# Two output halves in two groups of PSUM partitions, or as alternate rows of one eight-lane sum: a decode block on one core

## The chip, the cores and the metric

The kernel runs on one core of a Trainium2 chip. The metric is the device time of one execution in microseconds; several executions are timed and their median is given. A profiled execution of the same program gives the trace from which the views below are read.

## What is computed

Four sequences each decode one token. The input x (4 x 640) is layer-normalized, goes through an attention block with a cache and through a gated MLP, and both results are added to x:

```python
xn = _layernorm(x)
# A: 32 heads of 128, 4096 cached positions for each of the 4 sequences
q = (xn @ wq)                                   # 640 x 4096
scores = einsum('bhqd,bhkd->bhqk', q, k_cache) * Dh ** -0.5
o = einsum('bhqk,bhkd->bhqd', softmax(scores), v_cache)
a = o.reshape(B, 1, 4096) @ wo                  # 4096 x 640
# B: F = 1728, Fh = 864
z = gelu(xn @ w_in)
g = w_sp * layernorm(z[..., Fh:]) + b_sp
b = (z[..., :Fh] * g) @ w_out                   # 864 x 640
out = x + a + b                                 # 4 x 640, bf16
```

All inputs are bf16. The two caches hold 134 MB each, so 282 MB are read for 5 KB of result.

## The kernel before

**Units.** The attention is cut into 16 units: four groups of eight heads (HG = 4), and four sequences in each. Unit u is group u // 4, sequence u % 4. A unit's K, 8.4 MB, is spread over 128 partitions and loaded in four quarters (NK = 4, a quarter is 64 rows of 128 on each partition); its V, again 8.4 MB, goes to one tile, v_all. K quarters live in a ring of seven places, k_ring. The projection weights wo of a head group (1.3 MB) are loaded into place 4 of that ring.

**One K quarter** (step n of 64) is multiplied by the broadcast query on VectorE (`product`, L514), folded once (`fold_half`, L520), summed further on TensorE by eight matmuls with the identity (`sums`, L529), and reduced on VectorE (`row_sums`, L542). After four quarters come the maximum (`head_max`, L551 to L558), the exponential on ScalarE (`exps`, L564) and the spreading of the weights by head (`by_head`, L575). The product with V is 64 matmuls for each unit (`weighted`, L599), their result is copied by ScalarE (`take`, L611) and sorted (`pick_unit`, L630).

**The order of the loads** is a list written out by hand. `pump()` issues them one after another on SP's queue as soon as the place that a load goes to has been given back; the code marks a place as busy or free when the instructions that use it have been put down, and the semaphores that follow from it are waited for by SP. The order of instructions on TensorE, VectorE, ScalarE and SP in the main part is that of the program; nothing is reordered.

**The output sum.** All contributions to the output are accumulated in one PSUM tile, out_ps, in one bank: x itself (two matmuls, L355), the MLP (`gmlp`, 20 matmuls at L480, ten terms in two halves of 320 columns, at step 2 of 64), and wo (`group_proj`, 16 matmuls at L668 for each of the four head groups, eight heads in two halves). A half is 320 of the 640 output columns. Half 0 is summed in partitions 0 to 3, half 1 in partitions 32 to 35, each with a stationary operand of four columns, one for each sequence.

**The end.** After the last unit's K comes its V in two parts: the first through `weighted`, the second directly as stationary operand, 128 small matmuls (L778), in four pieces that arrive one after the other. Then VectorE divides by the sums (L786, into o_n_last), `group_proj` adds the last eight heads, whose wo arrives in six pieces (heads 0 and 1, 2 and 3, 4 and 5, 6, and the two halves of 7), ScalarE copies out_ps to SBUF as bf16 (L792), and two stores of four rows of 640 bytes go out, one on ScalarE's queue (L793), one on SP's (L794).

Of the kernel before, what the change touches and what calls it, by code (L numbers as in the profile page):

```python
# [9 lines left out]
FP32 = mybir.dt.float32  # L10
BF16 = mybir.dt.bfloat16
ACT = mybir.ActivationFunctionType
ALU = mybir.AluOpType
# [4 lines left out]
def kernel(  # L18
# [14 lines left out]
    nc = tc.nc  # L33
    P = nc.NUM_PARTITIONS
    Bsz, Sq, D = A_x.shape
# [12 lines left out]
    NQ = P // QD  # L48
    HT = 8
    PAR = HT // NQ  # L50
    LN = P // HT
    HG = H // HT
# [12 lines left out]
    NFC = NFF + FR  # L65
    LS = 5
    NOH = D // 2
# [4 lines left out]
    JR = Dh // QH  # L72
# [5 lines left out]
    const = ctx.enter_context(tc.tile_pool(name="const", bufs=1))  # L78
    work = ctx.enter_context(tc.tile_pool(name="work", bufs=1))
    small = ctx.enter_context(tc.tile_pool(name="small", bufs=2))  # L80
    once = ctx.enter_context(tc.tile_pool(name="once", bufs=1))
# [5 lines left out]
    ps_out = ctx.enter_context(tc.tile_pool(name="ps_out", bufs=1, space=PSUM))  # L87
# [133 lines left out]
    ident = const.tile([P, P], BF16)  # L221
# [3 lines left out]
    for e in range(PAR):  # L225
        nc.gpsimd.tensor_copy(
            out=of_row[:, e, :, :, e, :],
            in_=ident[:].rearrange("p (k q) -> p q k", q=QD)[:, 0:Bsz, :, None].to_broadcast(
                [P, Bsz, NQ, LN]
            ),  # L230
# [15 lines left out]
    for i in range(NSTAT):  # L246
# [5 lines left out]
        out=rstd[:], in_=mv[:, 1:2], func=ACT.Sqrt, bias=eps_tile[:Bsz], scale=1.0  # L252
# [4 lines left out]
        out=xn_bf[:],  # L257
        in0=x_bf[:],
# [11 lines left out]
    for c in range(DC):  # L270
        nc.tensor.transpose(
            out=xnT_ps[:, c, :], in_=xn_v[:, c, :], identity=ident[:Bsz, :Bsz]
# [8 lines left out]
    for e in range(PAR):  # L281
        q_ps = ps_pv.tile([P, HG, Dh], FP32, tag="pv", name="q_ps")
        for c in range(DC):
            for k in range(NQ):
                nc.tensor.matmul(  # L285
                    out=q_ps[k * QD : (k + 1) * QD],
# [58 lines left out]
        op1=ALU.add,  # L345
    )

    out_ps = ps_out.tile([P, NOH], FP32)
    OG = 32

    def out_sum(half):
        return out_ps[OG * half : OG * half + Bsz, :]

    for half in range(2):
        nc.tensor.matmul(  # L355
            out=out_ps[OG * half : OG * half + OG, :],
            lhsT=ident[:Bsz, :OG],
            rhs=x_bf[:, half * NOH : (half + 1) * NOH],
            start=True,
            stop=False,  # L360
        )

# [4 lines left out]
    nc.gpsimd.memset(gm["zz"][:], 0.0)  # L367
    gm["st"] = work.tile([1, 5 * Bsz], FP32, name="st")
    gm["ac"] = work.tile([1, 2 * Bsz], FP32, name="ac")
    gm["yT"] = work.tile([P, NFC, Bsz], BF16, name="yT")  # L370

    def gmlp():
        zz, gw, gt, gz = (gm[n] for n in ("zz", "gw", "gt", "gz"))
# [97 lines left out]
            in1=ac_sb[:, None, Bsz : 2 * Bsz].to_broadcast([P, NFC, Bsz]),  # L471
            op=ALU.add,
        )
        nc.vector.tensor_tensor(out=gm["yT"][:], in0=gz[:, 0, :, :], in1=sq, op=ALU.mult)
        w_terms = [w_out_sb[:, k] for k in range(NV)] + [w_row_sb]
        w_terms += [w_end_sb[:FT, r] for r in range(FR)]
        for k in range(NFC):
            w = P if k < NFF else FT
            for half in range(2):
                nc.tensor.matmul(  # L480
                    out=out_sum(half),
                    lhsT=gm["yT"][:w, k, :],
                    rhs=w_terms[k][:, half * NOH : (half + 1) * NOH],
                    start=False,
                    stop=False,
                )
# [151 lines left out]
    def group_turn(hg):  # L638
        rden = small.tile([P, 1], FP32, name="rden")
        nc.vector.reciprocal(out=rden[:], in_=rdens.pop(hg)[:])  # L640


        o_q = gr.pop(hg)[:].rearrange("p (q j) -> p q j", j=JR)
        o_n = once.tile([P, JR, PAR, QH], BF16, name="o_n")
        for e in range(PAR):
            nc.vector.scalar_tensor_tensor(  # L646
                out=o_n[:, :, e, :].rearrange("p j q -> p q j"),
                in0=o_q,
                scalar=rden[:, 0:1],
                in1=of_set[:, e : e + 1, None].to_broadcast([P, QH, JR]),  # L650
                op0=ALU.mult,
                op1=ALU.mult,
            )
        o_t = once.tile([P, JR, QD], BF16, name="o_t")
        nc.vector.transpose(
            out=o_t[:].rearrange("p j q -> p (j q)"),
            in_=o_n[:].rearrange("p j e q -> p (j e q)"),
        )
        o_s = once.tile([P, JR, Bsz], BF16, name="o_s")
        nc.vector.tensor_tensor(  # L660
            out=o_s[:], in0=o_t[:, :, 0:Bsz], in1=o_t[:, :, Bsz : 2 * Bsz], op=ALU.add
        )
        gr[hg] = [o_s[:, j, :] for j in range(JR)]

    def group_proj(hg):
        for n, o in enumerate(gr.pop(hg)):
            for half in range(2):
                nc.tensor.matmul(  # L668
                    out=out_sum(half),
                    lhsT=o,  # L670
                    rhs=wo_sb[:, n, half * NOH : (half + 1) * NOH],
                    start=False,
                    stop=(hg == HG - 1 and n == HT - 1),
                )
        busy.remove(WO_AT)

# [25 lines left out]
    with tc.manual_schedule(engines={E.PE, E.DVE, E.Activation, E.SP}):  # L702
        stage_q(0)
        nc.scalar.dma_start(out=wsp_bf[:], in_=B_w_sp[0:1, 0:1])
        nc.scalar.dma_start(out=bsp_bf[:], in_=B_b_sp[0:1].rearrange("(a b) -> a b", a=1))
        waiting = None
        mlp = gmlp()
        for n in range(NK * NU):
            u, i = divmod(n, NK)
            product(n)  # L710
            if n in (1, 2):
                next(mlp)
            if n:
                row_sums(n - 1)
            if i == 0 and u:
                head_max(u - 1)
                if waiting in taken:
                    picked(waiting)
            fold_half(n)
            if n == 1:  # L720
                next(mlp)
            if n in (1, 2):
                next(mlp)
            if i == 0 and u:
                exps(u - 1)
                if waiting in pvs:
                    take(waiting)
                by_head(u - 1)
            sums(n)
            if i == 0 and u + 1 < NU:  # L730
                stage_q(u + 1)
            if i == 0 and waiting is not None:
                if waiting in taken:
                    picked(waiting)
                if waiting % Bsz == Bsz - 1:
                    group_turn(waiting // Bsz)
                    group_proj(waiting // Bsz)
                waiting = None
            if n == 0:
                next(mlp)  # L740
            if n == 2:
                busy.remove(V)
            if n in turns:
                w = waiting = turns[n]
                if w % Bsz == Bsz - 1:
                    group_den(w // Bsz)
                if w == NU - 3:
                    weighted(w, v_runs[:, 0:NC], more=True)
                    weighted(w, v_runs[:, NC:NR], NG // 2)
                else:  # L750
                    weighted(w, v_runs)
                if i < NK - 1:
                    take(w)
                busy.remove(V)
            pump()
        weighted(NU - 2, v_runs)
        row_sums(NK * NU - 1)
        head_max(NU - 1)
        exps(NU - 1)
        take(NU - 2)  # L760
        by_head(NU - 1)
        den = ps_m.tile([P, NQ, PAR, Bsz], FP32, tag="m", name="den_all")
        nc.tensor.matmul(
            out=den[:],
            lhsT=ones_sq[:],
            rhs=acc[(HG - 1) % NACC][:, :, 0 : PAR * Bsz],
            start=True,
            stop=True,
        )
        rden = small.tile([P, NQ, PAR, Bsz], FP32, name="rden_all")  # L770
        nc.vector.reciprocal(out=rden[:], in_=den[:])
        picked(NU - 2)
        u, b = NU - 1, Bsz - 1
        weighted(u, v_ends[0])
        take(u)
        pick_last(u, more=True)
        for c in range(NC):
            nc.tensor.matmul(  # L778
                out=o_last[0][:, :, :, b],
                lhsT=v_ends[1][:, c, :],  # L780
                rhs=p_m[:, u % 2, NG // 2 + c // CB, c % CB, :].rearrange("p (k e) -> p k e", e=PAR),
                start=False,
                stop=(c == NC - 1),
            )
        o_n = small.tile([P, NQ, PAR, Bsz], BF16, name="o_n_last")
        nc.vector.tensor_tensor(out=o_n[:], in0=o_last[0][:], in1=rden[:], op=ALU.mult)  # L786
        gr[HG - 1] = [o_n[:, h // PAR, h % PAR, :] for h in range(HT)]
        group_proj(HG - 1)

        res = work.tile([P, NOH], BF16, name="res")  # L790
        out_v = out.flatten_outer_dims()
        nc.scalar.copy(out=res[0 : OG + Bsz], in_=out_ps[0 : OG + Bsz])  # L792
        nc.scalar.dma_start(out=out_v[:, 0:NOH], in_=res[0:Bsz])  # L793
        nc.sync.dma_start(out=out_v[:, NOH:D], in_=res[OG : OG + Bsz])  # L794


# [28 lines left out]
```

## Time and profile before

| | |
|---|---|
| median of 3 runs | 662.36 us (662.22 to 663.16) |
| span of the profiled execution | 660.5 us; the page gives no time outside the span |
| granted TensorE clock, mean | 0.694 |
| TensorE busy with matmuls | 310.9 us (47%) |
| VectorE busy | 524.9 us (79%) |
| bytes moved by DMA | 282.56 MB, mean 428 GB/s |
| L668 in the tail | 16 matmuls, 654.73 to 657.64 us |
| L480 | 20 matmuls, 55.39 to 58.31 us |

The page gives, for each engine, busy time, share of the span and number of instructions. PE is TensorE's matmuls, PEld its weight loads, DVE VectorE, ACT ScalarE, POOL GpSimd, SP the engine whose queue issues most loads. "ACTq" and "SPq" are the instructions that issue DMAs. The rows of digits cut the span in 40 equal slices and give the busy share of each in tenths. In the timeline a line is: start, length, engine, source line, operation, tiles written and read, shapes, count, and in brackets the idle time before it with what ended that time. In the answers for windows the columns are: the stretch, its length, the busy time of PE, PEld, DVE, ACT and POOL (with counts), the granted TensorE clock, the busy share of the DMA engines, and GB/s.

### The profile page before, as it was taken

Reading aid. Unit: us, or ns where it says so; the run is one execution under the profiler, and the core shown is the slowest. Engines: PE = TensorE matmul, PEld = TensorE weight load, DVE = VectorE, ACT = ScalarE, POOL = GpSimd, SP = SyncE. Lnnn points to the kernel's source line nnn. Section 1 sums busy time; section 2 is a strip of 40 time slices with the busy share of each in tenths; the row PEclk is TensorE's granted clock in tenths of the full one; section 3 lists DMA queues with packets and bytes.
Section 4 is the critical chain, followed back from the end, with each engine's and each line's share of the span. In section 5 each row is a group of like instructions: output and inputs, shape, how many; then the busy total and the mean of one; then the engine's idle time right before and its main releaser. Section 6 shows DMA issues by size and latency. Waiting matters only on the chain.

```text
span 660.5 us, 4704 instructions
## 1 busy us (share of the span) xinstructions
PE 310.9 (47%) x2035; PEld 135.7 (21%) x2035; DVE 524.9 (79%) x332; ACT 29.8 (5%) x73; POOL 2.7 (0%) x12
## 2 busy tenths in 40 slices
PE   0274363526527362472536336362462633736366
PEld 0131122212203121130212112121130221212124
DVE  2578988959598795969959598695969969999950
ACT  0020000000000000000000000000000000000000
POOL 1000000000000000000000000000000000000000
PEclk9756686766768677576767768677576767678765
DMA  9999999999999999999999999999999999999997
GB/s 372 435 448 429 430 441 437 438 425 437 430 433 438 433 433 438 433 434 425 437 437 438 421 433 438 441 438 433 429 426 441 430 433 445 411 428 437 457 400 281
DMA packets 8113, 282.56 MB, mean 428 GB/s; under 512 B 888, under 2 KB 2180, under 8 KB 2588
## 3 DMA queue, kind: packets, MB, share of 16 engines
q1 hardware_dynamic: 8024, 282.12, 99.0%
q8 instruction: 16, 0.26, 0.1%
q10 hardware_dynamic: 68, 0.13, 0.1%
q14 instruction: 5, 0.04, 0.0%
HBM read 282.24 MB, written 0.01 MB: 427 GB/s over the span
## 4 chain that ended last, share of the span: by engine, by line
DMA 60%; DVE 30%; PE 9%; issue 1%; ACT 0%; DVEq 0%; SPq 0%
DMA k_ring<-in_A_k_cache_dram 52%; DVE k_ring L514 15%; DVE k_ring L520 8%; PE s_ps L529 7%; DMA v_all<-in_A_v_cache_dram 4%; DMA k_ring<-in_A_wo_dram 3%; DVE s_sb L542 2%; DVE p_m L575 1%; DVE m L551 1%; PE out_ps L668 1%; DVE o_n L646 1%; PE zT L380 1%; PE pv L599 1%; DVE mt L553 0%; PE out_ps L480 0%
## 5 line engine op out<-in xcount | busy, mean ns | idle before, releaser
L514 DVE TENSOR_TENSOR k_ring<-k_ring,qbc 128x8192 bf16<-128x8192 bf16 x64 | 282.7, 4418 | 86.3 <-DMA k_ring<-in_A_k_cache_dram 86.3
L529 PE MATMUL s_ps<-k_ring,ident 128*128 128x512 bf16 x512 | 201.1, 564 | 313.7 <-DVE k_ring L520 313.5
L529 PEld LDWEIGHTS <-ident 128*128 128x128 bf16 x512 | 65.4, 129 | 427.7 <-issue 383.7
L520 DVE TENSOR_TENSOR k_ring<-k_ring 128x4096 bf16<-128x4096 bf16 x64 | 145.9, 2279 | 0.0
L599 PE MATMUL pv<-v_all,p_m 128*32 128x512 bf16 x960 | 60.2, 407 | 0.0
L542 DVE TENSOR_REDUCE s_sb<-s_ps 128x64 f32<-128x512 f32 x64 | 43.6, 682 | 5.7 <-PE s_ps L529 5.7
L575 DVE TENSOR_TENSOR p_m<-p_c,own 128x2048 bf16<-128x2048 bf16 x16 | 36.5, 2284 | 0.7 <-ACT p_c L564 0.7
L599 PEld LDWEIGHTS <-p_m 128*32 128x32 bf16 x992 | 25.8, 103 | 39.4 <-issue 17.1
L564 ACT ACTIVATE p_c<-s_sb,nm 128x256 bf16<-128x256 f32 x16 | 8.1, 508 | 331.2 <-DVE nm L558 331.2
L630 PEld LDWEIGHTS o_ps<-o_rows,pick 128*128 128x128 f32 x96 | 19.5, 280 | 4.1 <-issue 3.0
L630 PE MATMUL o_ps<-o_rows,pick 128*128 128x128 f32 x96 | 18.6, 357 | 0.0
L611 ACT COPY o_rows<-pv 128x512 f32<-128x512 f32 x16 | 9.4, 586 | 167.4 <-PE pv L599 167.4
L293 DVE TENSOR_SCALAR q_rows<-q_ps 128x512 bf16<-128x512 f32 x2 | 1.4, 692 | 12.3 <-PE q_ps L285 12.3
L786 DVE TENSOR_TENSOR o_n_last<-o_last,rden_all 128x32 bf16<-128x32 f32 x1 | 0.2, 192 | 12.3 <-PE o_last L778 12.3
L504 ACT CAST qbc<-qbc_ps 128x128 bf16<-128x128 f32 x16 | 4.3, 266 | 101.7 <-PE qbc_ps L496 101.7
L285 PE MATMUL q_ps<-v_all,xnT 128*32 128x512 bf16 x40 | 4.3, 618 | 8.9 <-DMA v_all<-in_A_wq_dram 8.9
L551 DVE TENSOR_REDUCE m<-s_sb 128x1 f32<-128x256 f32 x16 | 6.7, 420 | 0.6
L496 PE MATMUL qbc_ps<-q_rows,of_row 128*128 128x128 bf16 x32 | 6.0, 277 | 0.6 <-DVE q_rows L293 0.6
L496 PEld LDWEIGHTS <-of_row 128*128 128x128 bf16 x32 | 4.2, 134 | 8.3 <-issue 7.8
L668 PE MATMUL out_ps<-k_ring,o_s 128*4 128x320 bf16 x48 | 4.4, 331 | 2.2 <-DVE o_s L660 2.2
L685 PE MATMUL o_last<-hot,o_rows 128*128 128x8 f32 x32 | 4.9, 280 | 0.7 <-ACT o_rows L611 0.7
L685 PEld LDWEIGHTS o_last<-hot,o_rows 128*128 128x128 f32 x32 | 4.8, 225 | 1.8 <-ACT o_rows L611 1.6
(89 smaller groups left out, 74.6 us busy)
## 6 DMA issues: line engine op xcount, KB each, us to landing
k_ring<-in_A_k_cache_dram SPq DMA_DIRECT2D x6, 4096.0 KB, 24.8
v_all<-in_A_v_cache_dram SPq DMA_DIRECT2D x2, 4096.0 KB, 28.8
v_all<-in_A_wq_dram SPq DMA_DIRECT2D x1, 5120.0 KB
k_ring<-in_A_v_cache_dram SPq DMA_DIRECT2D x1, 4096.0 KB
k_ring<-in_A_wo_dram SPq DMA_DIRECT2D x3, 1280.0 KB, 20.1
v_all<-in_B_w_in_dram SPq DMA_DIRECT2D x1, 2160.0 KB
k_ring<-in_A_v_cache_dram SPq DMA_DIRECT2D x1, 2048.0 KB
k_ring<-in_A_v_cache_dram SPq DMA_DIRECT2D x1, 1024.0 KB
```

Source lines behind the costliest of these rows:

```text
L496: nc.tensor.matmul(out=qb_ps[:], lhsT=of_row[:, e, b].rearrange("p k f l -> p (k f l)"), rhs=q_rows[e][:, hg, :], start=(e == 0), stop=(e ...
L514: nc.vector.tensor_tensor(out=t, in0=t, in1=qbcs[u][:, None, :].to_broadcast([P, HC, Dh]), op=ALU.mult)
L520: nc.vector.tensor_tensor(out=t[:, :, 0:HD2], in0=t[:, :, 0:HD2], in1=t[:, :, HD2:Dh], op=ALU.add)
L529: nc.tensor.matmul(out=s[:], lhsT=ident[:], rhs=t[:, :, g * RW : (g + 1) * RW], start=(g == 0), stop=(g == m - 1),)
L542: nc.vector.tensor_reduce(out=scores[u][:, r * HC : (r + 1) * HC], in_=sums_ps.pop(n)[:], axis=AX.X, op=ALU.add,)
L551: nc.vector.tensor_reduce(out=m1[:], in_=scores[u][:], axis=AX.X, op=ALU.max)
L575: nc.vector.tensor_tensor(out=p_m[:, u % 2], in0=p_c.pop(u)[:].rearrange("p (g c) -> p g c", c=CB)[:, :, :, None].to_broadcast([P, NG, CB, HT]
L599: nc.tensor.matmul(out=pvs[u][cg * QD : (cg + 1) * QD, :], lhsT=p_m[:, u % 2, g0 + n].rearrange("p c h -> p (c h)"), rhs=v_at[:, n * CB : ...
L611: nc.scalar.copy(out=o[:].rearrange("p c d -> p (c d)"), in_=pvs.pop(u)[:])
L630: nc.tensor.matmul(out=gr[hg][:], lhsT=pick[:, c, Bsz - 1 - b : P + Bsz - 1 - b], rhs=o[:, c, :], start=(b == 0 and c == 0), stop=(b == Bs ...
L668: nc.tensor.matmul(out=out_sum(half), lhsT=o, rhs=wo_sb[:, n, half * NOH : (half + 1) * NOH], start=False, stop=(hg == HG - 1 and n == HT ...
L685: nc.tensor.matmul(out=o_last[0][:, :, :, u % Bsz], lhsT=o[:, c, :], rhs=hot[:, c, :].rearrange("p (k e) -> p k e", e=PAR), start=(c == 0) ...
```

## The change

The two halves become alternate rows of one sum over eight partitions: row 2b is half 0 of sequence b, row 2b + 1 is half 1. To put a term of four columns into the rows of one half, the stationary operand is interleaved with zeros: it is stored as nine columns, of which the odd ones hold the four values and the even ones zero, and `at_half` cuts out eight of them, from column 1 for half 0 and from column 0 for half 1. Every matmul of the output sum, as many as before, so writes all eight partitions, and adds zero to the rows of the other half.

The interleaved operands are three constant tiles, zeroed once by GpSimd: x_at (the identity's four columns), yT (the MLP's terms) and o_s (a head group's attention results, for all four groups; o_n_last is gone). VectorE writes its results into every second column of them. The first matmul of the sum alone starts it, and only the last one ends it. At the end there is one copy of eight partitions and one store of eight rows of 640 bytes, on ScalarE's queue; SP issues no store. Lines after the change are numbered six higher from `gmlp` to the steps of a K quarter, L674 is what L668 was.

```diff
-    out_ps = ps_out.tile([P, NOH], FP32)
-    OG = 32
-
-    def out_sum(half):
-        return out_ps[OG * half : OG * half + Bsz, :]
-
+    OR = 2 * Bsz
+    out_ps = ps_out.tile([OR, NOH], FP32)
+
+    def at_half(w, half):
+        return w[:, 1 - half : 1 - half + OR]
+
+    x_at = const.tile([Bsz, OR + 1], BF16, name="x_at")
+    nc.gpsimd.memset(x_at[:], 0.0)
+    nc.gpsimd.tensor_copy(out=x_at[:, 1::2], in_=ident[:Bsz, :Bsz])
+    yT = const.tile([P, NFC, OR + 1], BF16, name="yT")
+    nc.gpsimd.memset(yT[:], 0.0)
+    o_s = const.tile([P, JR, OR + 1], BF16, name="o_s")
+    nc.gpsimd.memset(o_s[:], 0.0)
     for half in range(2):
         nc.tensor.matmul(
-            out=out_ps[OG * half : OG * half + OG, :],
-            lhsT=ident[:Bsz, :OG],
+            out=out_ps[:],
+            lhsT=at_half(x_at, half),
             rhs=x_bf[:, half * NOH : (half + 1) * NOH],
-            start=True,
+            start=(half == 0),
             stop=False,
         )
...
-        nc.vector.tensor_tensor(out=gm["yT"][:], in0=gz[:, 0, :, :], in1=sq, op=ALU.mult)
+        nc.vector.tensor_tensor(out=yT[:, :, 1::2], in0=gz[:, 0, :, :], in1=sq, op=ALU.mult)
...
                 nc.tensor.matmul(
-                    out=out_sum(half),
-                    lhsT=gm["yT"][:w, k, :],
+                    out=out_ps[:],
+                    lhsT=at_half(yT[:w, k], half),
                     rhs=w_terms[k][:, half * NOH : (half + 1) * NOH],
...
-        o_s = once.tile([P, JR, Bsz], BF16, name="o_s")
         nc.vector.tensor_tensor(
-            out=o_s[:], in0=o_t[:, :, 0:Bsz], in1=o_t[:, :, Bsz : 2 * Bsz], op=ALU.add
-        )
-        gr[hg] = [o_s[:, j, :] for j in range(JR)]
+            out=o_s[:, :, 1::2], in0=o_t[:, :, 0:Bsz], in1=o_t[:, :, Bsz : 2 * Bsz], op=ALU.add
+        )
+        gr[hg] = [o_s[:, j] for j in range(JR)]
...
                 nc.tensor.matmul(
-                    out=out_sum(half),
-                    lhsT=o,
+                    out=out_ps[:],
+                    lhsT=at_half(o, half),
                     rhs=wo_sb[:, n, half * NOH : (half + 1) * NOH],
                     start=False,
-                    stop=(hg == HG - 1 and n == HT - 1),
+                    stop=(hg == HG - 1 and n == HT - 1 and half == 1),
                 )
...
-        o_n = small.tile([P, NQ, PAR, Bsz], BF16, name="o_n_last")
-        nc.vector.tensor_tensor(out=o_n[:], in0=o_last[0][:], in1=rden[:], op=ALU.mult)
-        gr[HG - 1] = [o_n[:, h // PAR, h % PAR, :] for h in range(HT)]
+        nc.vector.tensor_tensor(
+            out=o_s[:, :, 1::2],
+            in0=o_last[0][:].rearrange("p k e b -> p (k e) b"),
+            in1=rden[:].rearrange("p k e b -> p (k e) b"),
+            op=ALU.mult,
+        )
+        gr[HG - 1] = [o_s[:, h] for h in range(HT)]
         group_proj(HG - 1)
...
-        res = work.tile([P, NOH], BF16, name="res")
-        out_v = out.flatten_outer_dims()
-        nc.scalar.copy(out=res[0 : OG + Bsz], in_=out_ps[0 : OG + Bsz])
-        nc.scalar.dma_start(out=out_v[:, 0:NOH], in_=res[0:Bsz])
-        nc.sync.dma_start(out=out_v[:, NOH:D], in_=res[OG : OG + Bsz])
+        res = work.tile([OR, NOH], BF16, name="res")
+        nc.scalar.copy(out=res[:], in_=out_ps[:])
+        nc.scalar.dma_start(
+            out=out.flatten_outer_dims().rearrange("b (h n) -> (b h) n", h=2), in_=res[:]
+        )
```

More of the change, by code (lines that the diff above doesn't have):

```diff
@@ L369 @@
     gm["ac"] = work.tile([1, 2 * Bsz], FP32, name="ac")
-    gm["yT"] = work.tile([P, NFC, Bsz], BF16, name="yT")
     def gmlp():
```

## The prediction

> **What bounds the kernel now.** First the page. The DMA row says that the 16 DMA engines are busy from the first slice to the last but one, and the queue rows that SP's own queue does it.
>
> ```profile
> span 660.5 us, 4704 instructions
> PE 310.9 (47%) x2035; PEld 135.7 (21%) x2035; DVE 524.9 (79%) x332; ACT 29.8 (5%) x73; POOL 2.7 (0%) x12
> DMA  9999999999999999999999999999999999999997
> q1 hardware_dynamic: 8024, 282.12, 99.0%
> ```
>
> So for some 655 us the time is set by 282 MB at about 434 GB/s (the trace's DMA records never fall below 95% in any microsecond from 3 to 654), and an edit counts in one of two ways: by letting the queue run dry, or by lengthening what follows the last bytes. The second is the tail. The chain of waits from 610 us on shows it:
>
> ```profile
> 634.36 21.95 DMA k_ring<-in_A_wo_dram
> 656.35 1.30 PE out_ps L668 x8
> 657.67 0.42 ACT res L792
> ```
>
> The timeline of the tail (start, length, engine, line, tiles, count) shows the sixteen matmuls that the change rewrites:
>
> ```profile
> 653.85 0.59 PE L778 MATMUL o_last<-p_m,k_ring 128*128 128x8 bf16 x16 [0.65 <-DMA k_ring<-in_A_v_cache_dram]
> 654.48 0.19 DVE L786 TENSOR_TENSOR o_n_last<-o_last,rden_all 128x32 bf16<-128x32 f32 x1 [12.33 <-PE o_last L778]
> 654.73 1.46 PE L668 MATMUL out_ps<-k_ring,o_n_last 128*4 128x320 bf16 x8 [0.28 <-DVE o_n_last L786]
> 656.35 1.28 PE L668 MATMUL out_ps<-k_ring,o_n_last 128*4 128x320 bf16 x8 [0.17 <-DMA k_ring<-in_A_wo_dram]
> 657.67 0.42 ACT L792 CAST res<-out_ps 36x320 bf16<-36x320 f32 x1 [10.38 <-PE out_ps L668]
> 658.12 0.34 SPq L794 DMA_DIRECT2D out_dram<-res  x1
> 658.12 0.28 ACTq L793 DMA_DIRECT2D out_dram<-res  x1
> ```
>
> Looked at more closely (the timeline at 654.6 to 654.74 us), the two halves of a head run side by side; and windows give the clock:
>
> ```profile
> 654.73 0.43 PE L668 MATMUL out_ps<-k_ring,o_n_last 128*4 128x320 bf16 x2 [0.28 <-DVE o_n_last L786]
> 652.00:655.30 3.30, 2.13 (x50) 1.50 (x48) 0.19 (x1) 0.00 (x0) 0.00 (x0) 0.50 0.93 341
> 655.40:658.80 3.40, 2.00 (x14) 0.71 (x11) 0.00 (x0) 0.42 (x1) 0.00 (x0) 0.50 0.18 61
> ```
>
> Two matmuls take 0.43 us together, as one does alone: the records start 3 ns apart. One writes partitions 0 to 3, the other 32 to 35, so they use different columns of the array. The granted clock is 0.50 throughout the tail.
>
> **The price of a pair.** Undisturbed pairs of L668 in the tail start at 656.57 and 656.84, 0.267 us apart. L529 confirms that this is the price of one stream, not of two: at clock 0.50 its 512 columns repeat every 0.427 us (weight loads at 625.97, 626.40, 626.82 us), 0.834 ns a column, which makes 0.267 us for 320. So today sixteen matmuls cost eight streams.
>
> **The tail after the change.** Both halves now write the same partitions 0 to 7, from the same columns of the array, with different weights. They can only follow each other: sixteen streams. The first starts at 654.73 as before (L778 and L786 are unchanged up to there). The first spacing is 0.22 (as between the first two pairs, 654.73 and 654.95), fourteen more are 14 x 0.267 = 3.74, so the last starts at 658.69; a record is 0.47 long (median of L668) and the copy follows 0.03 later: 659.19 instead of 657.67, **+1.52 us**. The pieces of wo no longer hold anything up: they land at 655.45, 656.31, 656.73, 656.95 and 657.17 us, and their first matmuls would be due at 655.75, 656.82, 657.88, 658.42 and 658.69. What was partly waiting for DMA becomes a pure TensorE tail.
>
> L786's product goes to every second element of o_s instead of a dense tile. No row shows that stride with these operands; the nearest, L660 (175 ns) and L786 itself (192 ns) on the same 32 elements a lane, bound it at -0.02 to +0.1 us. I take 0. Weights of 8 columns for 4: the loads (80 to 129 ns) lie under the stream before, in the pairs as in L529. I take 0 here too.
>
> **A rule against that zero.** At the full granted clock (the group turn at 389 us) eight pairs, each with two loads of about 91 ns, take 1.25 us in all: seven steps of 0.136 and one record of 0.30, which leaves no room for a load between streams, though pair after pair uses the same rows and columns. The Trainium skill, TensorE: Matmul & The Clock Gate, Part 3 (The mechanism), says that a weight load overlaps running matmuls only where the row group differs, which would put every load here on the path. By that rule, with a load of 0.08 to 0.13, the sum would be 1.2 to 1.9 us more; by the row it is nothing.
>
> **Copy and store.** The copy stays at 320 elements a lane, 0.42 us, whether 36 or 8 lanes. Two stores of four rows become one of eight on ScalarE's queue. The old ones were issued at 658.12; ScalarE's landed at 659.41, SP's at 659.59, and SP, which collects all semaphores at the end, waited for it until 659.61. With one store it would be through at about 659.49 (0.06 for each further wait): **-0.12 us**. Bounds: if eight rows take SP's 1.47 us rather than ScalarE's 1.29, nothing is gained; 0.2 worse is my far end, an estimate of one such difference again. SP has nothing queued behind the removed store but the end.
>
> **Ahead of the tail.** All this is hidden, and its cover is as follows.
> - POOL gets four small operations (x_at, yT, o_s; its rows of that size are 0.10 to 0.21 us), at most 0.8 in sum, and the x matmuls (L355, at 2.29 us) now wait until about 4. Next on PE is L271 at 7.24, and after that the wq load at 16.45. Without that cover it would cost 0.8.
> - The MLP's twenty matmuls (L480) start at 55.39 and the next L529 at 58.24. Ten more streams at clock 0.50 are +2.67. Behind them stand L529 (so DVE's L542 at 61.75, and through DVE's order the K load that SP issues at 76.58), and, for the ten that read v_all, the V load issued at 56.92 (+1.3). What hides it is what the queue still holds: bytes issued less bytes moved are 2.49 MB at 56.92 and 2.16 MB at 76.58, 5.7 and 5.0 us at 434 GB/s. Left over: 4.4 and 2.3 us.
> - The three group turns (L668 at 230.87, 389.11, 547.55 us; 1.85, 1.25 and 1.25 us) grow by 1.1 to 2.1 us each. SP's K loads at 232.76 and 390.40 follow them, with 3.14 and 3.21 MB still queued (7.2 and 7.4 us).
> - L474 and L660 write with a stride: at most 0.1 us each, on DVE, which waits 86.3 us for K anyway.
>
> **Sum.** 1.52 - 0.12 = +1.40 us on a span of 660.5. The page gives no time outside the span; the median of the three runs is 662.36, 1.9 us above it, and I carry the difference over: **663.76 us**. About 0.2% (1.32 us) is what a measurement of this kernel can tell from no change, so the forecast lies right above that edge.
>
> **Rivals.**
> 1. *The clock is granted within the tail.* The trace's clock changes only at steps of 3.41 us; of the stretches at 0.50 in which matmul records filled 77% or more, 41 of 46 were followed by 1.00, of the emptier ones none. Sixteen streams in a row fill such a stretch. For: that. Against: in this run the boundaries are at 655.38 and 658.80, the second too late. If another run has one at 657.2, the remaining streams run twice as fast and 0.85 us is saved; later, less. Time 662.9 to 663.7. The Trainium skill, the same page, Part 1, calls this window free-running; only several runs could show that.
> 2. *Full clock through the whole tail: not slower.* If the grant comes before 656.0, the streams gain all that serializing costs. From the start at 1.00, sixteen take 16 x 0.136 = 2.2 us, until 656.9, and the last waits for wo at 657.17: copy at about 657.54 instead of 657.67, and with the store 662.1 us. Against: the stretch from 648.6 was 88% full of L685 and L778 and was still followed by 0.50.
> 3. *Exposed weight loads,* the mechanism weighed above: 665.0 to 665.7. Against: the row at 389 us.
> 4. *The queue runs dry* after the MLP, because more than the 2.3 us left over is lost between 55 and 77: every us beyond it is 1 us of time, 664.5 to 666. Against: DVE catches up, since a unit's work of 32.8 us (four each of L514, L520 and L542 are 29.5, L575 and L551 to L558 3.3) stands against 38.7 us of transfer (16.8 MB).
> 5. *The halves still overlap:* nothing but the store, 662.2. Against: no row has two matmuls at once on the same partitions.
>
> **Chances.** Forecast 0.66 (663.4 to 664.2, with runs 0.5 us apart); rival 1: 0.14; 2: 0.07; 3: 0.06; 4: 0.05; 5: 0.02. The range 662.8 to 664.7 holds the forecast, rival 1 and the near end of 4; it leaves out 2, 3, 5 and most of 4, together 0.18. Slower by over 0.2%: two thirds of the forecast (0.44) with 3 and 4, 0.55. Within it: the rest of the forecast (0.22), 1 and most of 2 and 5: 0.43. Faster: 0.02, scatter in 2 and 5.
>
> **What would show it.** In the changed kernel's timeline the tail should have sixteen L668-type matmuls starting 0.267 us apart at clock 0.50, about 4.4 us from first start to copy instead of 2.94, with no wait for wo among them; the MLP's twenty should last about 5.5 instead of 2.9 us; the DMA row should stay at 9, and the last wo piece should land at the same time within 0.5 us. Spacings of 0.35 or more mean rival 3; a clock of 1.00 in the windows of the tail means 1 or 2; a slice under 9 in the DMA row means 4; starts 3 ns apart mean 5. The forecast is wrong if the copy starts less than 1 us later after the last V piece than it does now.

## The result and the profile after

The changed kernel takes **664.12 us** (median of 8 runs, 663.06 to 665.41) against 662.35 us before (8 runs, 662.22 to 663.16): ratio 1.0024, 95% interval 1.0015 to 1.0033, 1.77 us slower. In the profile the line numbers above apply, except that L668 has become L673, not L674. The profiled execution has a span of 661.3 us and is the fastest of the eight (663.06), which matters below.

The page first: span, engines and the DMA row after the change.

```profile
span 661.3 us, 4706 instructions
...
PE 318.1 (48%) x2035; PEld 139.4 (21%) x2035; DVE 525.0 (79%) x332; ACT 29.8 (5%) x73; POOL 3.0 (0%) x16
...
DMA  9999999999999999999999999999999999999996
```

TensorE does as many matmuls and is busy 7 us longer. In tenths, the DMA row looks untouched. The chain of waits of the tail has changed its owner: no step of it is a transfer of wo any more.

```profile
612.01 42.01 DMA k_ring<-in_A_v_cache_dram
...
654.06 0.61 PE o_last L783 x16
...
654.95 3.64 PE out_ps L673 x16
...
658.61 0.41 ACT res L800
```

The windows of the tail (length, then busy PE, PEld, DVE, ACT, POOL, then the granted clock, DMA share and GB/s) show why it is 3.64 us and not 4.4:

```profile
654.90:657.60 2.70, 2.65 (x11) 1.30 (x12) 0.00 (x0) 0.00 (x0) 0.00 (x0) 0.50 0.47 162
657.60:658.60 1.00, 0.98 (x7) 0.44 (x5) 0.00 (x0) 0.00 (x0) 0.00 (x0) 1.00 0.00 0
```

The single records of the trace start 0.267 us apart until 657.57 and 0.136 apart from 657.73 on: the clock was granted within the tail, at 657.61. The timeline has the MLP and the loads behind it:

```profile
55.36 2.83 PE L486 MATMUL out_ps<-v_all,yT 128*8 128x320 bf16 x10 [2.94 <-DVE yT L480]
57.98 2.96 PE L486 MATMUL out_ps<-p_m,yT 128*8 128x320 bf16 x10
58.22 0.33 SPq L157 DMA_DIRECT2D v_all<-in_A_v_cache_dram  x1
60.88 3.27 PE L535 MATMUL s_ps<-k_ring,ident 128*128 128x512 bf16 x8
...
79.02 0.33 SPq L146 DMA_DIRECT2D k_ring<-in_A_k_cache_dram  x1
```

The MLP ends 2.6 us later, the V load is issued at 58.22 instead of 56.92 and the K load at 79.02 instead of 76.58, as worked out.

### The profile page after: what moved, and what is told of

Read it like the earlier page. It is cut to its first block, busy times and chain, and to the rows that moved or that the text cites. A ratio compares the mean times of both kernels' runs of the same rounds, so it can differ in the third digit from the quotient of the medians.

```text
span 661.3 us, 4706 instructions
## 1 busy us (share of the span) xinstructions
PE 318.1 (48%) x2035; PEld 139.4 (21%) x2035; DVE 525.0 (79%) x332; ACT 29.8 (5%) x73; POOL 3.0 (0%) x16
## 4 chain that ended last, share of the span: by engine, by line
DMA 58%; DVE 31%; PE 10%; issue 1%; SPq 0%; ACT 0%; DVEq 0%
DMA k_ring<-in_A_k_cache_dram 52%; DVE k_ring L520 15%; DVE k_ring L526 8%; PE s_ps L535 7%; DMA k_ring<-in_A_v_cache_dram 6%; DVE s_sb L548 2%; DVE p_m L581 1%; PE out_ps L673 1%; DVE m L557 1%; PE out_ps L486 1%; PE zT L386 1%; DVE o_n L652 1%; DVE mt L559 1%; DVE mt L562 0%; DVE nm L564 0%
## 5 line engine op out<-in xcount | busy, mean ns | idle before, releaser
L535 PE MATMUL s_ps<-k_ring,ident 128*128 128x512 bf16 x512 | 201.5, 564 | 306.7 <-DVE k_ring L526 306.6
L535 PEld LDWEIGHTS <-ident 128*128 128x128 bf16 x512 | 65.5, 130 | 421.3 <-issue 380.4
L673 PE MATMUL out_ps<-k_ring,o_s 128*8 128x320 bf16 x64 | 11.0, 332 | 2.5 <-DVE o_s L665 2.2
L673 PEld LDWEIGHTS <-o_s 128*8 128x8 bf16 x64 | 5.8, 95 | 7.2 <-DVE o_s L665 2.9
L783 PE MATMUL o_last<-p_m,k_ring 128*128 128x8 bf16 x128 | 4.0, 172 | 1.3 <-DMA k_ring<-in_A_v_cache_dram 1.3
```

The lines of the kernel that those rows point to most:

```text
L535: nc.tensor.matmul(out=s[:], lhsT=ident[:], rhs=t[:, :, g * RW : (g + 1) * RW], start=(g == 0), stop=(g == m - 1),)
L673: nc.tensor.matmul(out=out_ps[:], lhsT=at_half(o, half), rhs=wo_sb[:, n, half * NOH : (half + 1) * NOH], start=False, stop=(hg == HG - 1 a ...
```

## How a profile is taken apart here

Each profile splits at two points: the last landing of wo (from the trace's record of the DMA semaphores) and the start of the copy. What lies before the first is the body, what lies between is the tail, what lies after is copy, store and end. All in us; medians from all timed runs of the kernel.

| kernel | wo landed | landing to copy | copy to end of span | median | ratio to before, 95% interval |
|---|---|---|---|---|---|
| before | 657.17 | 0.50 | 2.81 | 662.35 | |
| after, first profile | 657.38 | 1.24 | 2.66 | 664.12 | 1.0024 (1.0015 to 1.0033) |
| again (after) | 657.64 | 1.78 | 2.66 | 664.03 | 1.0026 (1.0016 to 1.0037) |
| cols | 657.15 | 0.51 | 3.41 | 662.86 | 1.0007 (0.9998 to 1.0016) |
| tail | 657.20 | 1.72 | 2.65 | 663.48 | 1.0015 (1.0006 to 1.0024) |
| body | 658.34 | 0.51 | 2.65 | 662.83 | 1.0006 (0.9998 to 1.0015) |
| mlp | 657.28 | 0.50 | 2.65 | 662.47 | 1.0001 (0.9992 to 1.0010) |
| turns | 657.36 | 0.51 | 2.65 | 662.10 | 0.9996 (0.9987 to 1.0005) |
| warm | 659.25 | 0.49 | 2.65 | 663.47 | 1.0016 (1.0008 to 1.0025) |
| two | 657.39 | 2.03 | 2.73 | 664.05, one run | |
| dose | 658.96 | 0.51 | 2.81 | 664.27 | 1.0034 (1.0023 to 1.0045) |
| tailwarm (tail again) | 657.19 | 1.43 | 2.65 | 663.05, one run | |
| tailwarm2 | 657.11 | 0.47 | 2.65 | 662.32 | 1.0003 (0.9994 to 1.0012) |
| best | 657.38 | 0.51 | 2.76 | 662.24 | 1.0001 (0.9993 to 1.0010) |

For best, landing and copy are taken at ScalarE's copy; VectorE's starts 0.05 us before it. The kernel before was run again beside each set of kernels, and the ratios are to those runs: medians of 662.36 us (again to body), 662.33 (mlp to two) and 662.27 (dose to best), with all 81 runs between 662.05 and 663.68. The intervals of single kernels reach about 0.6 us to either side, so effects smaller than that are read from the columns, each of one profile, not from the ratios. One caution belongs to the first column: without any change in the body, wo landed anywhere from 657.11 to 657.38 (tailwarm2, best), so a landing 0.2 us later shows nothing.

## Experiments: tail or body

Two theories stood against each other. First: the tail alone, sixteen streams instead of eight. Second: the body too, because 1.77 us is more than the 1.40 of the sum, and the runs after the change lie far apart.

**again**, the changed kernel unchanged.

> The changed kernel unchanged, for a second profile and more times. First theory (the tail alone): the sixteen matmuls start 0.267 us apart at clock 0.50 and the median is 1.4 us above the kernel before, up to 0.85 us less where the clock is granted within the tail. Second theory (tail and body): the last piece of wo also lands later than in the kernel before (657.17 us there), by 0.3 to 1 us, and the median is 1.7 us or more above it. In the first profile it landed at 657.38, 0.2 later.

Median 664.03 (662.95 to 665.94). Its timeline:

```profile
655.24 4.15 PE L673 MATMUL out_ps<-k_ring,o_s 128*8 128x320 bf16 x16 [0.29 <-DVE o_s L790]
659.42 0.41 ACT L800 CAST res<-out_ps 8x320 bf16<-8x320 f32 x1 [11.30 <-PE out_ps L673]
```

The same sixteen matmuls take 4.15 us here (the grant came at 658.96, so that only the last two gained by it), and wo landed 0.47 later than before the change. So both parts move, and both vary from run to run.

**cols**, the interleaved operands with the halves side by side again.

```diff
 # OG is 32; out_sum(g) is out_ps[OG * g : OG * g + OR, :]
-                    out=out_ps[:],
+                    out=out_sum(half),
...
-        nc.scalar.copy(out=res[:], in_=out_ps[:])
...
+        nc.scalar.copy(out=res[0 : OG + OR], in_=out_ps[0 : OG + OR])
+        nc.scalar.dma_start(out=out_v[:, 0:NOH], in_=res[0:OR:2])
+        nc.sync.dma_start(out=out_v[:, NOH:D], in_=res[OG + 1 : OG + OR : 2])
```

> Interleaved weights of eight columns, zeros included, are kept, but half 1 is summed in partitions 32 to 39 again, and there are two stores as in the kernel before. Both theories: pairs start some 3 ns apart again and the time is that of the kernel before within 0.2 us (662.35). The rival that the interleaved, strided operands or the constant tiles themselves cost something: 0.3 us or more above it.

```profile
654.71 1.46 PE L678 MATMUL out_ps<-k_ring,o_s 128*8 128x320 bf16 x8 [0.29 <-DVE o_s L795]
656.34 1.27 PE L678 MATMUL out_ps<-k_ring,o_s 128*8 128x320 bf16 x8 [0.17 <-DMA k_ring<-in_A_wo_dram]
657.65 0.42 ACT L806 CAST res<-out_ps 40x320 bf16<-40x320 f32 x1 [9.34 <-PE out_ps L678]
658.10 0.74 SPq L808 DMA_DIRECT2D out_dram<-res  x1
658.10 0.66 ACTq L807 DMA_DIRECT2D out_dram<-res  x1
```

Up to the copy this is the kernel before to within 0.03 us: weights of eight columns, the stride of o_s and the constant tiles cost nothing on the path. The 0.5 us of the median are not theirs either. They stand behind the copy (3.41 us to the end, not 2.81) and belong to the two stores, which here read every second partition and take 0.66 and 0.74 us to issue instead of 0.28 and 0.34. That was a flaw of this kernel, not of the change.

**tail** and **body**: serial in one part only. The start flags that go with the edit are left out here.

```diff
 # group_proj; out_sum(g) is out_ps[32 * g : 32 * g + OR, :]
-                    out=out_ps[:],
+                    out=out_sum(0 if hg == HG - 1 else half),   # tail
+                    out=out_sum(half if hg == HG - 1 else 0),   # body
 # x and the MLP: out_sum(half) in tail, out_sum(0) in body
```

> Serial in the tail only: x, the MLP and the first three head groups add half 1 in partitions 32 to 39 (which is never read, so these terms are left out of half 1's rows), and the last group adds both halves in partitions 0 to 7. One store. First theory: as the changed kernel, 1.4 us above the kernel before at clock 0.50 (0.5 to 1.4 with a grant in the tail). Second theory: 0.3 to 1 us faster than the changed kernel run beside it, and the runs lie closer together.

> Serial in the body only: everything up to the third head group is summed in partitions 0 to 7 as in the changed kernel, and the last group adds its half 1 in partitions 32 to 39 (never read, so that this term is left out of half 1's rows). One store. First theory: the time of the kernel before less 0.1 us for the store, 662.2 us. Second theory: 0.3 to 1 us above the kernel before, with more scatter, and the last piece of wo lands later by that much.

The tail kernel first, then the body kernel:

```profile
654.77 4.12 PE L678 MATMUL out_ps<-k_ring,o_s 128*8 128x320 bf16 x16 [0.29 <-DVE o_s L795]
658.92 0.41 ACT L805 CAST res<-out_ps 8x320 bf16<-8x320 f32 x1 [11.21 <-PE out_ps L678]
```

```profile
657.55 1.26 PE L678 MATMUL out_ps<-k_ring,o_s 128*8 128x320 bf16 x8 [0.19 <-DMA k_ring<-in_A_wo_dram]
658.85 0.41 ACT L805 CAST res<-out_ps 8x320 bf16<-8x320 f32 x1 [9.25 <-PE out_ps L678]
```

Both medians lie above the kernel before: +1.12 us (runs from 662.76 to 664.31) for the tail, +0.47 (662.06 to 664.18) for the body. The body's interval still includes 1, so its price rests on the landing and on the next section. Each of the two contains the saving at the copy and the store, 0.16; counted once, they add up to 1.12 + 0.47 + 0.16 = 1.75 us, as much as the 1.67 to 1.77 measured. That the sum fits so well is more than intervals of 0.6 us can promise. In the profiles the separation is clean: the tail kernel's wo lands at 657.20 as before and the copy follows 1.72 later; the body kernel's copy follows 0.51 after the landing as before, but the landing is at 658.34, 1.17 later.

## Experiments: why the body loses

**mlp** and **turns** split the body further (the same edit: everything but x and the MLP side by side, or everything but the first three groups).

> Serial in x and the MLP only; the four head groups add half 1 in partitions 32 to 39 (never read, so their terms are left out of half 1's rows). One store. First theory (the MLP's ten extra streams thin the load queue early on, some of the 16 DMA engines run short, and that is never made up): 0.3 to 0.6 us above the kernel before, scattered as the body-only kernel (median 0.47 above), with DMA records lost between 55 and 100 us. Rival (the group turns do it): 662.2 us, 0.1 below, and close together.

> Serial in the first three head groups only; x, the MLP and the last group add half 1 in partitions 32 to 39 (never read, so these terms are left out of half 1's rows). One store. First theory (the MLP): 662.2 us, 0.1 below the kernel before, close together. Rival (the turns): 0.3 us or more above it, scattered.

The turns kernel is the fastest of all (662.10) and lies close together (662.00 to 662.73): the group turns cost nothing that can be seen. The MLP kernel has a median of 662.47, only 0.14 above before, less than expected, but reaches 663.60. Its profile caught a run of little loss. With the store's 0.16 added back, the MLP costs 0.30 and the turns -0.07, where the body as a whole cost 0.63; the 0.4 between is within the intervals and is not accounted for. So the medians alone don't pin the loss on the MLP; the DMA records show where it arises.

Summed over the 16 engines, this is the busy time lost against the kernel before in two stretches, beside the moments of the two issues and the backlog then (us; bytes issued less the bytes of finished packets, at 434 GB/s, as in the prediction). Losses are engine-us: 1 is one of the 16 engines idle for a microsecond.

| profile | V issue, backlog | lost 56 to 66 | K issue, backlog | lost 76 to 90 |
|---|---|---|---|---|
| before | 56.9, 5.7 | 0 | 76.6, 5.0 | 0 |
| tail, turns, cols, tailwarm, tailwarm2, best | 56.8 to 57.2, 5.1 to 5.9 | 0 | 76.3 to 77.0, 4.8 to 5.4 | 0 |
| mlp | 58.1, 4.8 | 0.7 | 76.4, 5.1 | 0 |
| again | 58.1, 4.8 | 0.9 | 76.3, 5.9 | 0 |
| two | 58.1, 4.8 | 1.1 | 76.6, 5.0 | 0 |
| after | 58.2, 4.8 | 0.4 | 79.0, 2.6 | 0.8 |
| body | 57.9, 4.8 | 1.1 | 78.6, 3.9 | 1.3 |
| warm | 57.9, 4.8 | 0.4 | 78.6, 3.0 | 2.1 |

All other stretches from 20 to 640 us agree within 0.2 in all of them. In quarters of a microsecond, the body kernel has about 15 of 16 engines busy from 60.75 to 61.75 and again from 80.5 to 81.75: one engine, or one after the other, is without work for about a microsecond. This little is not averaged away: the 2.4 engine-us that the body kernel lost would be 0.15 us spread over 16 engines, but wo landed 1.17 later. Smaller losses can hardly be told from the landing: "after" lost 1.2 and landed wo at 657.38, as did best, which lost nothing; again lost 0.9 and landed it at 657.64.

The backlog column is too high, and this hides the rule. A packet of 64 KB takes 2.4 us here, and the column counts the packets that are under way as if nothing of them had moved. With their part taken off in proportion, the kernel before had 4.6 and 4.3 us left at the two issues, not 5.7 and 5.0. Every issue with a loss then had 3.4 us or less left (3.2 to 3.4 for the V loads, 1.9 to 2.5 for the K loads), and every issue without one 3.8 or more. In the kernels with a serial MLP all 16 engines were busy again only 2.7 to 3.8 us after the issue, so what was left ran out on some engine before the new load was there.

The K load is late in some runs and not in others because part of the MLP and L535 behind it run at full clock in some. From 56 to 66 us the granted clock is 0.62 in "after" and 0.84 in "again":

```profile
56.00:66.00 10.00, 8.15 (x27) 2.99 (x25) 5.44 (x3) 0.00 (x0) 0.00 (x0) 0.62 0.98 419
56.00:66.00 10.00, 7.02 (x32) 2.98 (x31) 7.96 (x4) 0.00 (x0) 0.00 (x0) 0.84 0.98 413
```

The eight matmuls of L535 behind the MLP (L540 in body and mlp) take 3.2 to 3.3 us in after, body and warm, whose K load is late, and 1.9 us in again, mlp and two, whose K load is not.

**dose** puts the suspected delay into the kernel before, for the V load over three times as long, without any other part of the change.

```diff
         for k in range(NFC):
+            if k == 1:
+                burn(12)      # 12 matmuls of 512 columns into a spare PSUM tile
```

> The kernel before, with 12 idle matmuls of 512 columns behind the MLP's first term; their sum is never read. They hold up the V load that SP issues at 56.9 us and the K load at 76.6 us by 2.6 to 5.1 us (clock 1.00 or 0.50), about twice as much as the serial MLP did (1.2 and up to 2.4). If a late load thins the queue until some DMA engines run short, the records lose several engine-us between 56 and 90 us, wo lands 0.5 to 2 us later than 657.17 and the median is 0.5 to 2 us above the kernel before. If the mean backlog (5.7 and 5.0 us) hides it, as predicted: no loss, 662.35.

```profile
55.32 0.43 PE L494 MATMUL out_ps<-v_all,yT 128*4 128x320 bf16 x2 [2.93 <-DVE yT L474]
...
56.51 4.15 PE L481 MATMUL hot_ps<-q_rows,ident 128*128 128x512 bf16 x10 [0.22 <-issue]
60.59 0.71 PE L494 MATMUL out_ps<-v_all,yT 128*4 128x320 bf16 x8
...
61.34 0.33 SPq L157 DMA_DIRECT2D v_all<-in_A_v_cache_dram  x1
...
78.77 0.33 SPq L146 DMA_DIRECT2D k_ring<-in_A_k_cache_dram  x1
```

The V load went out 4.4 us late, on a backlog of 1.1 us (0.3 with the packets under way taken off), and 18 engine-us were lost from 60.75 to 63; in the quarter of a microsecond after 62.0 only one engine of 16 was busy. wo landed 1.8 us later, with the tail untouched (0.51), and the median is 2.00 us above before. The K load was 2.2 us late, less than expected; with its backlog back at 5.0 (3.8), it lost nothing. So a late load in this place does cost, and by this way: the delay alone, without any other part of the change, brings the loss and the later landing.

## Experiments: what the tail's price is made of

**warm** and **tailwarm2** put idle matmuls into TensorE's waits of the tail, in the changed kernel and in the tail-only one; **tailwarm** is the tail-only kernel once more.

```diff
+        burn(6)
         weighted(u, v_ends[0])
+        burn(3)
         take(u)
...
+            burn({63: 2, 95: 1, 111: 3, 127: 1}.get(c, 0))   # behind L783's pieces
```

> The changed kernel, with 16 idle matmuls of 512 columns put into TensorE's waits of the tail (6 before the first part of the last V, 3 behind it, 2, 1, 3 and 1 behind the pieces of the second); their sum is never read. If the clock is what makes sixteen streams longer than the wait for wo, it is granted at 1.00 in the tail, the matmuls start 0.136 us apart until they wait for wo, and the copy starts within 0.4 us of the last landing of wo; the median is then 1.0 to 1.6 us below the changed kernel run beside the same kernel before, that is 0.1 to 0.7 above that one (the body's 0.5 stays). If serial streams cost for another reason (their weight loads, the same partitions), the spacing stays at 0.27 and the time at 1.6 us above.

> The tail-only serial kernel once more, one look beside its warmed variant: as before, about 1.7 us from the last landing of wo to the copy at clock 0.50, less with a grant in the tail.

> Serial in the tail only (half 1's other terms left out, as in the tail-only kernel), with 16 idle matmuls of 512 columns in TensorE's waits of the tail, whose sum is never read. If streams times clock are the price of the tail, the clock is at 1.00 there, the copy starts 0.5 us after the last landing of wo as in the kernel before, and the median is 662.2 to 662.5, against 663.48 without the idle matmuls. If not, 663.3 or more.

The timeline of tailwarm2 and the windows of its tail come first; those of the kernel "two", whose profile had no grant in its tail, follow.

```profile
654.64 1.49 PE L678 MATMUL out_ps<-k_ring,o_s 128*8 128x320 bf16 x8
656.30 1.25 PE L678 MATMUL out_ps<-k_ring,o_s 128*8 128x320 bf16 x8 [0.17 <-DMA k_ring<-in_A_wo_dram]
657.58 0.42 ACT L820 CAST res<-out_ps 8x320 bf16<-8x320 f32 x1 [9.79 <-PE out_ps L678]
```

```profile
651.00:654.60 3.60, 3.20 (x69) 2.00 (x69) 0.20 (x1) 0.00 (x0) 0.00 (x0) 1.00 0.99 376
654.60:657.60 3.00, 2.66 (x16) 1.30 (x16) 0.00 (x0) 0.02 (x1) 0.00 (x0) 1.00 0.38 130
```

The same two views of "two":

```profile
654.96 4.43 PE L673 MATMUL out_ps<-k_ring,o_s 128*8 128x320 bf16 x16 [0.29 <-DVE o_s L790]
659.43 0.42 ACT L800 CAST res<-out_ps 8x320 bf16<-8x320 f32 x1 [10.86 <-PE out_ps L673]
```

```profile
655.00:659.40 4.40, 4.39 (x16) 1.85 (x16) 0.00 (x0) 0.00 (x0) 0.00 (x0) 0.50 0.23 79
```

At clock 1.00 the same sixteen serial matmuls wait for wo again and the copy follows 0.47 after its landing; at 0.50 they take 4.43 and the copy follows 2.03 after. With the idle matmuls alone the tail-only kernel falls from 663.48 (1.12 above the kernel before beside it) to 662.32 (0.05 above). So the tail's price is streams times clock; no other cost of serial streams shows. In warm, the tail is cured as well (0.49), but that profile had the greatest loss in the body of the kernels with a serial MLP (wo at 659.25), and its median of 663.47, 1.1 above before, is above the 0.1 to 0.7 that were expected; the tail's clock in its other runs is not recorded, and the excess stays open.

**two**, two stores again instead of one: 2.73 us from copy to end, between 2.81 and 2.66.

> The changed kernel with two stores of four rows, one on each queue, as before. From the start of the copy to the end of the span the kernel before took 2.81 us, the changed one 2.66 in both profiles. If the single store is what saves 0.15 us, this kernel takes 2.75 to 2.85; if the smaller copy does, 2.66.

So the single store accounts for about half of the 0.15 us; what the other half is stays open. **best**, meant to beat both:

```diff
-        nc.scalar.copy(out=res[0 : OG + Bsz], in_=out_ps[0 : OG + Bsz])
-        nc.scalar.dma_start(out=out_v[:, 0:NOH], in_=res[0:Bsz])
-        nc.sync.dma_start(out=out_v[:, NOH:D], in_=res[OG : OG + Bsz])
+        res = x_bf
+        nc.vector.tensor_copy(out=res[:, 0:NOH], in_=out_sum(0))
+        nc.scalar.copy(out=res[:, NOH:D], in_=out_sum(1))
+        nc.scalar.dma_start(out=out.flatten_outer_dims(), in_=res[:])
```

> A version meant to beat both: the kernel before with its halves side by side, each copied at the end on an engine of its own (half 0 on VectorE, half 1 on ScalarE) into four rows of 640, and one store of four rows on ScalarE's queue. If the single store is worth what the copy-to-end times say (2.65 against 2.81 us), 662.2 us, 0.15 below the kernel before; if not, 662.35.

662.24 beside 662.27: no difference that can be told. VectorE's copy takes 0.48 us and the store is issued 0.50 after ScalarE's copy starts, not 0.45; from ScalarE's copy to the end it saves 0.05 (2.76 against 2.81).

## Why the prediction was right, and where its steps were off

- **The tail, +1.52 at clock 0.50: right.** In the one profile without a grant ("two") the first start to the copy takes 4.46 us, 1.52 more than the 2.95 of before. Spacing 0.267, no wait for wo, the start 0.89 us after the first matmul on the last V piece (0.88 before): as worked out.
- **The weight loads: hidden, as the row said.** In the changed kernel a load of 131 ns starts 2 ns after the matmul before it and the next matmul follows at 0.267 us; at full clock a load of 88 ns does, and the next matmul follows at 0.136. These are the times of 320 columns alone. The rule of the Trainium skill (TensorE: Matmul & The Clock Gate, Part 3, The mechanism) that loads overlap running matmuls only with another row group does not hold here; the measurement decides. The same section also lets a load run ahead into a background weight buffer, which would agree; no trace here shows that buffer.
- **Rival 1, the grant within the tail: it came in four of five profiles, where it was given 0.14.** Of the five profiles with an unwarmed serial tail, four had a grant in it (657.61, 658.96, 658.44 and 657.82 us) and one just after (659.99). Sixteen streams fill a stretch of 3.41 us by themselves; only where its boundary lies is chance. That the boundaries lie elsewhere in every run agrees with the Trainium skill, the same page, Part 1, which calls the window free-running. By the profiles the grants take 0.3 to 0.8 us off the 1.52 in these four. The step that failed is reading one run's boundaries as those of the others. The first profile even meets the prediction's own sign of being wrong, that the copy starts less than 1 us later after the last V piece: from the first matmul on that piece (L778 before, L783 after) to the copy it takes 4.55 us instead of 3.82, only 0.73 longer. In again and two it takes 1.25 and 1.53 longer.
- **Copy and store, -0.12: measured -0.15.** The size was right, the reason half so: "two" gives the single store 0.07, and the rest stays open.
- **"Left over: 4.4 and 2.3 us" in the body: the step that failed.** The predicted moments of issue were right (58.2 and 79.0 in the first profile), and so, counted in the same way, were the backlogs, nearly (4.8 and 2.6). But the count took packets under way as still to move in full, so that only 3.2 and 1.9 us were really left, a mean over 16 engines, and the new load needed up to 3.8 us to keep all of them busy. One of them ran short before the mean was used up. The body was put at 0 and costs about 0.6 us by the medians (0.47 and the store's 0.16), with a wide scatter; it is rival 4, which sets in earlier than the prediction let it. The sign that was to show it, a slice under 9 in the DMA row, could not: the body kernel's 2.4 engine-us are under 1% of a slice's 264.
- **Partly luck.** The two errors have opposite signs, about -0.25 for grants in the median of the tail-only kernel (1.52 - 0.15 - 1.12) and +0.6 for the body, so the median came only 0.37 above the forecast. The mechanism of the tail was right; that the time lay so near the sum is owed to the errors partly cancelling.

## What to carry to other kernels

Two small matmuls that write different groups of 32 PSUM partitions cost one stream here; merging their outputs into one group doubles the streams, whatever it saves in copies and stores, and what that costs depends on where in the kernel it stands and on the granted clock at that moment. Where a kernel is bound by one load queue, a delay is not hidden until the mean backlog is used up: here an issue with 3.4 us or less left cost something and one with 3.8 or more did not. Take what has moved of the packets under way off the backlog, and look at the DMA records by quarter microseconds, since tenths per slice show nothing. Read a clock window's phase in one profile as chance, and price a burst both with and without a grant.

## What was not expected of the hardware

- Some DMA engine idled 2.5 to 3.0 us after the next load had been issued (V at 58.2, an engine missing from 60.75 to 61.25 in "after"). Shares of a load land up to 2 us apart (61.1 to 63.1 for the third K load of the kernel before), which explains why one engine runs out before the others; why the new load's share had not reached it by then is open, and so is why in dose, where nearly all engines had run out, all were busy again 1.9 us after the issue.
- Stores of four rows from every second partition took 0.66 to 0.74 us to issue and the span ended 0.6 us later than with adjacent partitions ("cols").
- Sixteen idle matmuls of 512 columns in waits, in the tail alone, were worth some 1.1 us of the median of the tail-only kernel (663.48 to 662.32, each beside its own runs of the kernel before: +1.12 to +0.05).
